# Second mixture of experts: where an expert's row transposes, its routing phase and spare matmuls stand in the queues

## Chip, core and metric

The program runs on one core of one Trainium2 chip. The metric is device time in microseconds (us) of one execution. The engines are named as in the profile: PE (TensorE, matmuls), DVE (VectorE), ACT (ScalarE), POOL (GpSimd) and SP (SyncE, which here only issues DMAs). Each engine runs its own instructions in the order in which they were queued, and waits at an instruction whose inputs are not there yet.

## What is computed

Three stages follow one another: attention, a first mixture of experts in which every token goes through all 8 experts, and a second mixture in which every token goes to one expert. Only the second mixture is touched by the change. Of the reference it is this part (N = 1152 tokens, D = 512, F = 1024, E = 8):

```python
def _moe2_ref(x, w_gate, w1, w2):
    cap = N // E                               # 144 tokens for each expert
    logits = x @ w_gate
    order = np.argsort(-logits.flatten())
    ...                                        # greedy: the best pair first; a token takes one expert,
    ...                                        # an expert takes at most cap tokens
    for e in range(E):
        mask = assigned == e
        h = np.maximum(x[mask] @ w1[e], 0.0)
        out[mask] = h @ w2[e]
```

## The kernel before

The last stage, `moe2`, works through the experts in the order in which they fill up. In this text "expert 0" is the one that fills first, and "phase p" is the routing that fills expert p. All of it is written as small operations that are handed to a planner (`Plan`); the planner keeps a model of times, always emits the operation that can start first by that model, and so fixes the order of the instructions on every engine. The operations have these names:

- `t`: the 36 last matmul groups of the first mixture (L689), whose sums DVE adds to `acc` and SP saves to the DRAM buffer `ysc`.
- Phase p, on DVE and PE in turn: `m` (each token's best open expert, L201 and L202); `bc0` to `bc2` (PE, L209: nine transposes that spread these values over the partitions); `oh` (DVE one-hots, L217 to L222); `cmp0` to `cmp8` (DVE, L229 to L232: nine compares of all tokens with all); `cnt0` to `cnt2` (PE, L241: three blocks of 27 narrow matmuls that count who stands ahead); `as`, `tot`, `close`, `left`, `sel` (who is in; which expert is full now); `pl` (PE, L302 and L304: each token's place in its expert); `spr` (DVE, L311 and L313: the one-hot matrix `hot`); `ix` (PE, L320: the token numbers in order); `ad` (DVE, L326 and L328: row addresses); `ga` (POOL, L338: two gathers of 72 rows, `xa` and `xb`, from `ysc`). `wlo` and `whi` load the expert's weights through SP (L358, L362).
- Expert p, on PE: `tin0` and `tin1` (L413, L414: transposes of the gathered rows, four each), 32 matmuls of the first layer (`h`, L422), 32 of the second (`y`, L432), `to0` and `to1` (L441: transposes back), and `sc` (POOL, L447: two scatters to `out`). ACT copies out of PSUM in between.

The main line is a list: the 36 `t`, then 64 matmuls for each expert. It is emitted in its own order. Everything else is fitted in between. `plan.mark` names a point of the main line, and an operation can be made to wait for it in the plan. Two such points matter here. Phase p may not begin (`m`) before the mark `("at", p)`, which is the main operation number HA + HB(p - 1) = 20 + 30(p - 1). And `tin0` and `tin1` of expert p wait for the gather and for `("h0", p - 1)`, which is the last matmul of the first 4 of the previous expert; from there on the planner may emit them as soon as its model says that the gather has landed. In that model a gather lands 0.9 + 1.5 us after its issue on POOL:

```python
op("m", [("close", p - 1), ("left", p - 1), ("at", p)] if p else [], ...)
op("ga", ["ad"] + ..., [("POOL", 2.1, 0.0), ("DMA", 0.9, 1.5)], gather)
op(f"tin{h}", ["ga"] + ... + ([("h0", p - 1)] if p else [("t", 35)]), ...)
plan.mark(("at", p), CFG["HA"] + CFG["HB"] * (p - 1))
```

The first gather needs all of `ysc`, so it comes after the last `t`. `ybank()` hands out four PSUM banks in turn to `t`, `tin`, `h`, `y` and `to`; `T` (three banks) serves the broadcasts and counts; `PV` is a single bank that `tot`, `pl` and `ix` share. The gathered rows have two buffers, so the gather of expert p also waits for `tin1` of expert p - 2.

Of the kernel before, what the change touches and what calls it, by code (L numbers as in the profile page):

```python
# [35 lines left out]
KT = D // 128  # L36
FB = F // 128
# [5 lines left out]
def tile_attention_moe_moe2(  # L43
# [44 lines left out]
    if dbg is not None and "acc" in dbg:  # L88
        m1.dbg = dbg["acc"]
        nc.sync.dma_start(dbg["lg"], lg)  # L90
    xst.close()
    moe2(tc, nc, ctx, ps, m1, w1b, w2b, ident, lg, ysc, out)


# [66 lines left out]
        return done  # L161


CFG = dict(CG=3, NCMP=6, HA=20, HB=30)


def moe2(tc, nc, ctx, ps, m1, w1b, w2b, ident, lg, ysc, out):
    BIG = 3.0e38
    FAR = 1.0e6
    if True:  # L170
# [3 lines left out]
        bef_b, edge, meta, ones_b = c2["bef_b"], c2["edge"], c2["meta"], c2["ones_b"]  # L174
        pen, u, rem, ac, spacer, tick = c2["pen"], c2["u"], c2["rem"], c2["ac"], c2["spacer"], c2["tick"]
        X = {}
# [3 lines left out]
        plan = Plan()  # L180
# [7 lines left out]
        S_ = {}  # L188

        def phase(p):  # L190
# [34 lines left out]
            def compare(j):  # L225
                g = two.tile([128, NT, 128], BF, name="cmp", bufs=CFG["NCMP"])
                mj = d["m"][:, j:j + 1]
                if j:
                    V.tensor_scalar(g[:, :j], d["mb"][:, :j], mj, None, op0=OP.is_lt)  # L229
                if j + 1 < NT:  # L230
                    V.tensor_scalar(g[:, j + 1:], d["mb"][:, j + 1:], mj, None, op0=OP.is_le)
                V.scalar_tensor_tensor(g[:, j], d["mb"][:, j], mj, edge, op0=OP.subtract, op1=OP.is_lt)  # L232
                d["g", j] = g
# [132 lines left out]
            def op(name, deps, segs, f, *a):  # L366
                plan.add((name, p), [x if isinstance(x, tuple) else (x, p) for x in deps], segs,
                         lambda: f(*a))

            if not last:  # L370
                op("m", [("close", p - 1), ("left", p - 1), ("at", p)] if p else [], [("DVE", 0.5, 0.15)], prefer)
                for c in range(3):
                    op(f"bc{c}", ["m"], [("PE", 0.33, 0.2)], bcast, c)
                    op(f"mb{c}", [f"bc{c}"], [("ACT", 0.37, 0.1)], bcopy, c)
                op("oh", ["m"], [("DVE", 1.35, 0.1)], onehot)
                mb = ["mb0", "mb1", "mb2"]
                for j in range(NT):
                    op(f"cmp{j}", mb, [("DVE", 1.12, 0.15)], compare, j)
                cg = CFG["CG"]
                js = [list(range(j, min(j + cg, NT))) for j in range(0, NT, cg)]  # L380
                for n, g in enumerate(js):
                    op(f"cnt{n}", ["oh"] + [f"cmp{j}" for j in g] + (["cnt0"] if n else []),
                       [("PE", 0.23 * len(g), 0.2)], count, g)
                op("as", [f"cnt{n}" for n in range(len(js))], [("DVE", 0.8, 0.1)], assign)
                op("tot", ["as"], [("PE", 0.04, 0.2)], total)
                op("left", ["as"], [("DVE", 0.4, 0.1)], left)
                op("close", ["tot"], [("DVE", 1.1, 0.1)], close)
                op("sel", ["close", "left"], [("DVE", 0.6, 0.1)], select)
            else:
                op("sel", [("sel", p - 1), ("left", p - 1)], [("DVE", 1.3, 0.1)], select)  # L390
# [4 lines left out]
            op("ix", ["spr"], [("PE", 1.0, 0.2)], index)  # L395
            op("ad", ["ix"], [("DVE", 0.5, 0.2)], address)
            op("ga", ["ad"] + ([("tin1", p - 2)] if p > 1 else []) + ([("ga", p - 1)] if p else [("save", t) for t in range(3, NT)]),
               [("POOL", 2.1, 0.0), ("DMA", 0.9, 1.5)], gather)
            op("whi", ["wlo", "ga"], [("SP", 0.3, 0), ("DMA", 7.0, 2.0)], weights, 4, 8)

        Z = {}
# [2 lines left out]
        def expert(p):  # L404
# [49 lines left out]
            def op(name, deps, segs, f, *a, main=False):  # L454
                plan.add((name, p), [x if isinstance(x, tuple) else (x, p) for x in deps], segs, lambda: f(*a), main)

            for h in range(2):
                op(f"tin{h}", ["ga"] + (["tin0"] if h else []) + ([("h0", p - 1)] if p else [("t", 35)]),
                   [("PE", 0.55, 0.2), ("ACT", 0.3, 0.15)], tin, h)
            for f in range(FB):  # L460
                for kt in range(KT):
# [11 lines left out]
        for n, (f, save) in enumerate(m1.tail()):  # L473
            plan.add(("t", n), [], [("PE", 0.645, 0.2)], f, main=True)
            if save:
                t, evac = save
                plan.add(("ev", t), [("t", n)], [("DVE", 0.67, 0.1)], evac)
                plan.add(("save", t), [("ev", t)], [("SP", 0.1, 0.0), ("DMA", 0.9, 1.6)], lambda t=t: m1.save(t))
        for p in range(E):
            phase(p)  # L480
            expert(p)
        for p in range(1, E):
            plan.mark(("at", p), CFG["HA"] + CFG["HB"] * (p - 1))
        plan.run()


# [1027 lines left out]
```

## Time and profile before

| | us |
|---|---|
| median of 3 runs | 1204.88 (1204.75 to 1207.76) |
| the profiled execution | 1208.25 |
| its span, first to last instruction | 1206.4 |
| mean granted clock of PE over the span | 0.976 of full speed |

The profile page gives for each engine its busy time, and in a view of windows the busy time of each engine in any stretch together with PEclk, the clock that was granted to TensorE as a share of full speed: 1.00 is 2.4 GHz and 0.50 is 1.2 GHz. In the timeline a bracket behind a row is the time for which the engine stood idle before it, and what it waited for. A matmul in full 32-bit precision stands in the trace as two records, so that 32 of them count as x64. The last `t` of the profiled execution ends at about 1000.6 us, the second mixture's own matmuls begin with the arrival of the first gather at 1009.24 us, and the last matmul of the last expert's second layer ends at about 1198 us.

### The profile page before, as it was taken

The numbers are of one execution on the slowest core, as the hardware profiler recorded it, in microseconds if no ns is written. First come the engines' busy times: TensorE is split into PE (matmuls) and PEld (weight loads), VectorE is DVE, ScalarE is ACT, GpSimd is POOL, SyncE is SP. The second block draws the span as 40 slices with busy tenths as digits, with TensorE's granted clock in tenths as the row PEclk, the third lists the DMA queues.
The fourth block names the chain that finished last, engine by engine and source line by source line (L and its number), as shares of the span: only waits on it lengthen the run. The fifth ranks groups of instructions, "written<-read, shape, count | busy, mean of one in ns | idle before, by whom it ended". The sixth has DMA issues, their size and how long they took to land.

```text
span 1206.4 us, 19849 instructions
## 1 busy us (share of the span) xinstructions
PE 1161.8 (96%) x7718; PEld 1048.2 (87%) x7719; DVE 788.4 (65%) x1710; ACT 415.5 (34%) x934; POOL 470.1 (39%) x428
## 2 busy tenths in 40 slices
PE   7999999999899999999999999999999997889997
PEld 4989888898889888898989898898978976889997
DVE  6999984365666666666666666658898676658300
ACT  4888885224332323233232323221211111112121
POOL 6787846215543444354345434331130001134411
PEclk8999999999899999999999999999999997879999
DMA  3232223200211121111112111241000027547930
GB/s 107 68 83 73 52 66 113 70 1 1 60 46 35 35 71 36 36 55 51 36 35 71 36 35 43 68 170 36 3 34 27 1 81 238 194 160 232 288 120 21
DMA packets 92765, 90.07 MB, mean 75 GB/s; under 512 B 26368, under 2 KB 65408, under 8 KB 92544
## 3 DMA queue, kind: packets, MB, share of 16 engines
q1 hardware_dynamic: 90336, 83.43, 22.0%
q0 software_dynamic: 2048, 4.72, 1.3%
q8 instruction: 61, 1.00, 0.4%
q10 hardware_dynamic: 288, 0.66, 0.2%
q14 instruction: 32, 0.26, 0.1%
HBM read 79.48 MB, written 4.72 MB: 70 GB/s over the span
## 4 chain that ended last, share of the span: by engine, by line
PE 81%; DVE 10%; DMA 2%; POOL 2%; issue 2%; ACT 2%; SPq 0%; POOLq 0%; DVEq 0%; ACTq 0%
PE Y L907 21%; PE T L849 18%; PE T L670 11%; PE Y L689 10%; PE T L1210 5%; PE Y L432 4%; PE Y L422 4%; PE PV L1304 3%; DVE junk L944 2%; DMA xb<-ysc,ix 2%; POOL xa L338 1%; PE S L1248 1%; PE S L1250 1%; DVE negmax L1252 1%; DVE al L1291 1%
## 5 line engine op out<-in xcount | busy, mean ns | idle before, releaser
L862 DVE TENSOR_TENSOR v<-T,v 128x256 f32<-128x256 f32 (+1 forms) x200 | 90.5, 453 | 75.8 <-PE T L849 74.5
L909 DVE SCALAR_TENSOR_TENSOR acc<-Y,pw,acc 128x512 f32<-128x512 f32 x180 | 132.3, 744 | 5.4 <-PE Y L907 2.6
L670 PE MATMUL T<-xH,wa 128*128 128x384 f32 x480 | 132.4, 337 | 0.0
L849 PE MATMUL T<-xH,wa 128*128 128x256 f32 (+1 forms) x480 | 115.4, 296 | 0.0
L849 PEld LDWEIGHTS T<-big,wb 128*128 128x128 f32 x720 | 104.3, 188 | 10.3 <-DVE v L862 3.3
L849 PE MATMUL T<-big,wb 128*128 128x256 f32 (+1 forms) x720 | 108.5, 294 | 3.1 <-DVE v L862 3.1
L689 PE MATMUL Y<-wb,hh 128*128 128x512 f32 x312 | 98.2, 396 | 1.6 <-ACT acc L696 1.6
L678 ACT ACTIVATE hh<-T 128x384 fp32r<-128x384 f32 x62 | 30.5, 492 | 185.5 <-PE T L670 185.3
L670 PEld LDWEIGHTS T<-xH,wa 128*128 128x128 f32 x480 | 87.6, 188 | 2.9
L849 PEld LDWEIGHTS T<-xH,wa 128*128 128x128 f32 x480 | 84.4, 190 | 5.1
L679 DVE SCALAR_TENSOR_TENSOR hl<-T,hh 128x384 fp32r<-128x384 f32 x62 | 34.5, 556 | 78.1 <-ACT hh L678 78.0
L670 PE MATMUL T<-xL,wa 128*128 128x384 f32 x240 | 80.6, 336 | 0.0
L849 PE MATMUL T<-xL,wa 128*128 128x256 f32 (+1 forms) x240 | 71.0, 296 | 0.0
L856 DVE SCALAR_TENSOR_TENSOR hlB<-v,hhB 128x320 fp32r<-128x320 f32 x60 | 47.5, 792 | 32.3 <-ACT hhB L855 32.3
L689 PEld LDWEIGHTS Y<-wb,hh 128*128 128x128 f32 x312 | 57.1, 188 | 11.3 <-ACT acc L696 2.1
L758 POOL TENSOR_TENSOR wa<-wraw,wa 128x512 fp32r<-128x512 f32 (+1 forms) x40 | 41.1, 1027 | 64.9 <-ACT wa L757 64.9
L777 POOL TENSOR_TENSOR wb<-wraw,wb 128x512 fp32r<-128x512 f32 x20 | 25.6, 1299 | 99.3 <-ACT wb L776 99.3
L855 ACT ACTIVATE hhB<-v 128x320 fp32r<-128x320 f32 x60 | 28.3, 472 | 104.2 <-DVE v L862 104.2
L1252 DVE TENSOR_REDUCE negmax<-S 128x1 f32<-128x576 f32 (+1 forms) x80 | 60.0, 751 | 5.4 <-PE S L1250 4.6
L777 POOL TENSOR_TENSOR wa<-wraw,wa 128x512 fp32r<-128x512 f32 x20 | 26.0, 1323 | 96.2 <-ACT wa L776 96.2
L907 PE MATMUL Y<-wa,hhB 128*128 128x512 f32 x200 | 62.9, 397 | 0.0
L907 PE MATMUL Y<-wb,hhB 128*128 128x512 f32 x200 | 62.8, 396 | 0.0
(290 smaller groups left out, 3057.5 us busy)
## 6 DMA issues: line engine op xcount, KB each, us to landing
wraw<-in_moe_w SPq DMA_DIRECT2D x56, 512.0 KB
big<-in_moe_w SPq DMA_DIRECT2D x22, 512.0 KB
wraw<-in_moe_w SPq DMA_DIRECT2D x40, 256.0 KB
wa<-in_moe_w SPq DMA_DIRECT2D x18, 512.0 KB
wb<-in_moe_w SPq DMA_DIRECT2D x12, 512.0 KB
hlk<-hlk SPq DMA_DIRECT2D x14, 320.0 KB
ysc<-acc SPq DMA_DIRECT2D x9, 256.0 KB
rawk<-in_k SPq DMA_DIRECT2D x16, 128.0 KB
```

Source lines behind the costliest of these rows:

```text
L422: nc.tensor.matmul(Z["ph"][:, f % 2], d["wa"][kt // 2][:, kt % 2, f * 128:(f + 1) * 128], Z["xg", p][:, kt], start=(kt == 0), stop=(kt == ...
L432: nc.tensor.matmul(Z["py"][:, b % 2], d["wb"][f // 4][:, f % 4, b * 128:(b + 1) * 128], Z["h", p][:, f], start=(f == 0), stop=(f == FB - 1))
L670: nc.tensor.matmul(p[:, :CH], w[:, wi, kt, (fb % 2) * 128:(fb % 2) * 128 + 128], x[:, kt, o], start=(n == 0), stop=(n == 11))
L689: nc.tensor.matmul(self.Y[c][t], a[:, o], w[:, wi, fb % 2], start=(fb == 0 and n == 0), stop=(fb == FB - 1 and n == 2))
L777: G.tensor_tensor(d["W"][:, 1, h], r[:, 2 + h], d["W"][:, 0, h].bitcast(F32), op=OP.subtract)
L849: nc.tensor.matmul(bank[:, 0:n], d[t][:, ww, b, r * 128:(r + 1) * 128], x(xw, r), start=(first and i == 0), stop=(i == 5), skip_group_chec ...
L856: V.scalar_tensor_tensor(HL[:, f, o], src, 0.0, HH[:, f, o].bitcast(F32), op0=OP.max, op1=OP.subtract)
L862: V.tensor_tensor(o, bank[:, 0:n], x, op=OP.add)
L907: nc.tensor.matmul(y, h[:, f, o], w[:, ww, f], start=(f == 0 and z == 0), stop=(f == 1 and z == 2))
L909: V.scalar_tensor_tensor(self.acc[:, t], y, self.pw[:, t, e:e + 1], self.acc[:, t], op0=OP.mult, op1=OP.add)
L1210: nc.tensor.transpose(o, i, ident[:n, :n])
L1252: nc.vector.tensor_reduce(m[0:n], p[0:n, :, :288], axis=AX.XY, op=OP.max, negate=True)
```

## The change

There are four edits, all in `moe2`:

- `("at", p)` stays for phase 1 alone. From phase 2 on a phase begins, in the plan, as soon as `close` and `left` of the phase before it are done.
- `tin0` and `tin1` of expert p > 0 wait for a new mark `("tn", p)` in place of `("h0", p - 1)`. It is the main operation 8 (LEAD) before expert p's first matmul, so the transposes stand among the last 7 matmuls of expert p - 1.
- The planner's model of a gather's flight is 5.0 us in place of 1.5 us for p > 0. This only moves operations.
- 24 matmuls `fill` (FILL) are put on the main line behind the last `t`: 128 x 512, bf16, stationary `ones_b`, moving the `hot` matrix of phase 0, all into one bank of `ybank()`. Nothing reads what they write.

```diff
--- before.py
+++ after.py
@@ -161,7 +161,7 @@
         return done
 
 
-CFG = dict(CG=3, NCMP=6, HA=20, HB=30)
+CFG = dict(CG=3, NCMP=6, HA=20, LEAD=8, FILL=24)
 
 
 def moe2(tc, nc, ctx, ps, m1, w1b, w2b, ident, lg, ysc, out):
@@ -368,7 +368,7 @@
                          lambda: f(*a))
 
             if not last:
-                op("m", [("close", p - 1), ("left", p - 1), ("at", p)] if p else [], [("DVE", 0.5, 0.15)], prefer)
+                op("m", [("close", p - 1), ("left", p - 1)] + ([("at", p)] if p == 1 else []) if p else [], [("DVE", 0.5, 0.15)], prefer)
                 for c in range(3):
                     op(f"bc{c}", ["m"], [("PE", 0.33, 0.2)], bcast, c)
                     op(f"mb{c}", [f"bc{c}"], [("ACT", 0.37, 0.1)], bcopy, c)
@@ -395,7 +395,7 @@
             op("ix", ["spr"], [("PE", 1.0, 0.2)], index)
             op("ad", ["ix"], [("DVE", 0.5, 0.2)], address)
             op("ga", ["ad"] + ([("tin1", p - 2)] if p > 1 else []) + ([("ga", p - 1)] if p else [("save", t) for t in range(3, NT)]),
-               [("POOL", 2.1, 0.0), ("DMA", 0.9, 1.5)], gather)
+               [("POOL", 2.1, 0.0), ("DMA", 0.9, 1.5 if p == 0 else 5.0)], gather)
             op("whi", ["wlo", "ga"], [("SP", 0.3, 0), ("DMA", 7.0, 2.0)], weights, 4, 8)
 
         Z = {}
@@ -455,7 +455,7 @@
                 plan.add((name, p), [x if isinstance(x, tuple) else (x, p) for x in deps], segs, lambda: f(*a), main)
 
             for h in range(2):
-                op(f"tin{h}", ["ga"] + (["tin0"] if h else []) + ([("h0", p - 1)] if p else [("t", 35)]),
+                op(f"tin{h}", ["ga"] + (["tin0"] if h else []) + ([("tn", p)] if p else [("t", 35)]),
                    [("PE", 0.55, 0.2), ("ACT", 0.3, 0.15)], tin, h)
             for f in range(FB):
                 for kt in range(KT):
@@ -476,11 +476,23 @@
                 t, evac = save
                 plan.add(("ev", t), [("t", n)], [("DVE", 0.67, 0.1)], evac)
                 plan.add(("save", t), [("ev", t)], [("SP", 0.1, 0.0), ("DMA", 0.9, 1.6)], lambda t=t: m1.save(t))
+        X["f"] = None
+
+        def fill():
+            if X["f"] is None:
+                X["f"] = m1.ybank()
+            nc.tensor.matmul(X["f"], ones_b, S_[0]["hot"].rearrange("p t c -> p (t c)")[:, 0:512],
+                             start=True, stop=True)
+
+        for i in range(CFG["FILL"]):
+            plan.add(("fill", i), [("spr", 0)], [("PE", 0.23, 0.0)], fill, main=True)
+        nf = len(plan.line)
         for p in range(E):
             phase(p)
             expert(p)
+        plan.mark(("at", 1), CFG["HA"])
         for p in range(1, E):
-            plan.mark(("at", p), CFG["HA"] + CFG["HB"] * (p - 1))
+            plan.mark(("tn", p), nf + 2 * FB * KT * p - CFG["LEAD"])
         plan.run()
```

All engines but PE keep their number of instructions; PE gets the 24 matmuls with their weight loads. The order moves from phase 1 on. Three places follow.

On PE, behind the last `t`, where the first gather is awaited. Before, the last count of phase 1 (L241) and its total (L256) are followed by the transposes of expert 0 (L413, L414):

```order
L241 LDWEIGHTS cmp_10184
L241 MATMUL T_10105<-oh_10020,cmp_10184 128x8
L256 LDWEIGHTS ones_b_2927
L256 MATMUL PV_10229<-a_10225,ones_b_2927 128x72
L413 MATMUL Y_10266<-ident_66,xa_10191 128x72
L414 MATMUL Y_10266<-ident_66,xb_10192 128x72
```

With the change the spare matmuls (L484) stand around the counts and the total: 3 ahead of the second count block, 14 ahead of the third, 5 behind it, and these last two behind the total:

```order
L256 LDWEIGHTS ones_b_2927
L256 MATMUL PV_10256<-a_10244,ones_b_2927 128x72
L484 LDWEIGHTS ones_b_2927
L484 MATMUL Y_10147<-hot_10032,ones_b_2927 128x512
L484 LDWEIGHTS ones_b_2927
L484 MATMUL Y_10147<-hot_10032,ones_b_2927 128x512
L413 MATMUL Y_10285<-ident_66,xa_10205 128x72
L414 MATMUL Y_10285<-ident_66,xb_10206 128x72
```

What moved: PE has 24 matmuls to run between the last `t` and the first transposes, of which 17 stand ahead of the third count block.

On PE, expert 1's transposes. Before, they stand in the first layer of expert 0 (L422), after 22 of its 32 matmuls, and the broadcast of phase 2 (L209) stands just ahead of them:

```order
L209 MATMUL T_10356<-ident_66,m_10339 128x128 x3
L209 MATMUL T_10360<-ident_66,m_10339 128x128 x3
L209 MATMUL T_10365<-ident_66,m_10339 128x128 x3
L422 MATMUL Y_10345<-xg_10265,wa_9986 128x144 x2
L422 MATMUL Y_10345<-xg_10265,big1_9985 128x144 x2
L413 MATMUL Y_10396<-ident_66,xa_10326 128x72
L414 MATMUL Y_10396<-ident_66,xb_10327 128x72
L413 MATMUL Y_10396<-ident_66,xa_10326 128x72
L414 MATMUL Y_10396<-ident_66,xb_10327 128x72
L422 MATMUL Y_10345<-xg_10265,wa_9986 128x144 x2
L422 MATMUL Y_10409<-xg_10265,big1_9985 128x144
```

With the change they stand in the second layer of expert 0 (L432), 7 matmuls before its end; ahead of them is the broadcast of phase 3, and between the two halves comes the index of expert 2 (L320):

```order
L209 MATMUL T_10635<-ident_66,m_10611 128x128 x3
L209 MATMUL T_10639<-ident_66,m_10611 128x128 x3
L209 MATMUL T_10644<-ident_66,m_10611 128x128 x3
L432 MATMUL Y_10607<-h_10344,wa_9988 128x144 x4
L432 MATMUL Y_10607<-h_10344,wa_9987 128x144
L413 MATMUL Y_10660<-ident_66,xa_10386 128x72
L414 MATMUL Y_10660<-ident_66,xb_10387 128x72
L413 MATMUL Y_10660<-ident_66,xa_10386 128x72
L414 MATMUL Y_10660<-ident_66,xb_10387 128x72
L320 LDWEIGHTS hot_10651
L320 MATMUL PV_10669<-meta_2925,hot_10651 72x4
```

What moved: 57 matmuls of expert 0 now stand ahead of expert 1's transposes, where 22 did, and the routing is a phase further on at that point. The same holds for the experts after it. Before, 30, 10, 4, 4, 4 and 4 of the 64 matmuls of the expert before stood ahead of the transposes of experts 2 to 7; with the change it is 57 for each.

On DVE, the address of expert 1 (L326, L328). Before, it comes right behind the one-hot matrix of expert 1 (L311, L313) and ahead of phase 2 (L201, L202):

```order
L311 SCALAR_TENSOR_TENSOR pos_10282<-sel_10246,PV_10272 128x9
L313 TENSOR_TENSOR hot_10284<-rc_2919,pos_10282 128x1296
L326 COPY idf_10318<-PV_10298 72x8
L328 SCALAR_TENSOR_TENSOR ix_10320<-idf_10318 72x4
L201 TENSOR_TENSOR lm_10338<-lg_73,pen_2929 128x72
L202 TENSOR_REDUCE m_10339<-lm_10338 128x9
```

With the change phase 2 has begun, and the address stands behind the first compare of phase 2 (L231, L232) with eight compares behind it:

```order
L220 TENSOR_TENSOR key_10336<-key_10336,km_10337 128x72
L222 TENSOR_TENSOR oh_10342<-key_10336,u_2931 128x72
L231 TENSOR_SCALAR cmp_10367<-mb_10301,m_10298 128x1024
L232 SCALAR_TENSOR_TENSOR cmp_10367<-mb_10301,m_10298,edge_2923 128x128
L326 COPY idf_10374<-PV_10348 72x8
L328 SCALAR_TENSOR_TENSOR ix_10376<-idf_10374 72x4
L229 TENSOR_SCALAR cmp_10380<-mb_10301,m_10298 128x128
```

What moved: the address of expert 1 now stands inside a run of compares, as the addresses of experts 2 to 5 do in both kernels. On POOL the gather of expert 2 now stands ahead of the scatter of expert 0, and the gather of expert 6 ahead of the scatter of expert 3; the rest of its sequence is the same.

## Rows read from the trace of the kernel before

**Rows 1.** Windows: stretch, us, busy of PE, PEld, DVE, ACT, POOL, PEclk, DMA share, GB/s
```profile
1009.24:1198.15 188.91, 176.56 (x1787) 173.73 (x1788) 81.92 (x277) 39.84 (x92) 49.69 (x48) 0.90 0.57 190
1198.15:1206.40 8.25, 1.23 (x10) 0.70 (x7) 0.00 (x0) 1.49 (x3) 1.96 (x3) 0.78 0.12 36
```

**Rows 2.** PE groups by line, 1009.24 to 1198.2: busy us, mean ns, idle before, releasers
```profile
L413 PE MATMUL Y<-ident,xa 72*128 72x72 f32 x31 | 7.2, 265 | 6.1 <-DMA xa<-ysc,ix 6.1
L414 PE MATMUL Y<-ident,xb 72*128 72x72 f32 x32 | 7.2, 272 | 6.0 <-DMA xb<-ysc,ix 6.0
L320 PE MATMUL PV<-meta,hot 128*72 128x4 bf16 x126 | 5.8, 178 | 1.1 <-DVE hot L313 1.1
```

**Rows 3.** PE timeline: start, us, what, [idle before, releaser]
```profile
1009.24 0.38 PE L414 MATMUL Y<-ident,xb 72*128 72x72 f32 x1 [0.92 <-DMA xb<-ysc,ix]
1023.54 0.28 PE L414 MATMUL Y<-ident,xb 72*128 72x72 f32 x1 [1.72 <-DMA xb<-ysc,ix]
1053.90 0.38 PE L414 MATMUL Y<-ident,xb 72*128 72x72 f32 x1 [2.67 <-DMA xb<-ysc,ix]
1078.94 0.35 PE L413 MATMUL Y<-ident,xa 72*128 72x72 f32 x1 [4.32 <-DMA xa<-ysc,ix]
```

**Rows 4.** Windows, columns as in rows 1: the five stretches at half clock
```profile
1009.24:1018.40 9.16, 9.16 (x62) 9.06 (x63) 3.53 (x11) 1.23 (x3) 1.97 (x2) 0.50 1.02 362
1025.20:1028.61 3.41, 3.41 (x40) 3.32 (x39) 3.41 (x11) 0.23 (x1) 0.00 (x0) 0.50 0.88 321
1053.90:1062.78 8.88, 8.88 (x64) 8.78 (x65) 3.58 (x21) 1.23 (x3) 0.32 (x1) 0.50 0.03 11
1079.72:1086.67 6.95, 6.95 (x56) 6.85 (x57) 1.90 (x11) 1.23 (x3) 0.73 (x2) 0.50 0.10 34
1131.04:1134.45 3.41, 3.41 (x16) 3.41 (x16) 0.34 (x2) 0.60 (x2) 2.58 (x3) 0.50 1.02 348
```

**Rows 5.** Windows, columns as in rows 1: the wait for the first gather
```profile
1000.60:1004.75 4.15, 2.19 (x55) 1.66 (x51) 3.83 (x10) 0.00 (x0) 0.06 (x1) 1.00 0.18 67
1004.75:1009.24 4.49, 0.63 (x3) 0.29 (x3) 2.85 (x16) 0.00 (x0) 2.44 (x4) 0.50 0.26 72
```

**Rows 6.** PE timeline: the last count ahead of the first gather's arrival
```profile
1004.22 0.44 PE L241 MATMUL T<-oh,cmp 128*128 128x8 bf16 x9 [0.46 <-DVE cmp L229]
```

**Rows 7.** PE timeline: the spare matmuls at the program's start
```profile
11.12 2.76 PE L1150 MATMUL PV<-wb 128*128 128x512 bf16 x6
18.07 1.04 PE L1150 MATMUL PV<-wb 128*128 128x512 bf16 x4
```

**Rows 8.** PE timeline: one sample of each block of the stage, at full clock
```profile
1173.75 8.00 PE L432 MATMUL Y<-h,wa 128*128 128x144 f32 x64
1064.05 1.15 PE L209 MATMUL T<-ident,m 128*128 128x128 f32 x9
1066.75 0.76 PE L320 MATMUL PV<-meta,hot 128*72 128x4 bf16 x18
1095.03 0.82 PE L241 MATMUL T<-oh,cmp 128*128 128x8 bf16 x27
```

**Rows 9.** DVE timeline: one routing phase, from its start to the next one's
```profile
1107.32 0.23 DVE L201 TENSOR_TENSOR lm<-lg,pen 128x72 f32<-128x72 f32 x1
1110.68 0.75 DVE L231 TENSOR_SCALAR cmp<-mb,m 128x1024 bf16<-128x1024 f32 x1
1121.98 0.23 DVE L249 TENSOR_TENSOR ok<-T,rem 128x72 f32<-128x72 f32 x1 [1.72 <-PE T L241]
1124.84 0.16 DVE L289 TENSOR_SCALAR new<-pen 128x8 f32<-128x8 f32 x1
```

**Rows 10.** POOL timeline: issues of gathers, columns as in rows 3
```profile
1044.18 1.13 POOL L338 DMA_INDIRECT xa<-ysc,ix  x1 [0.55 <-issue]
1069.06 7.28 POOL L338 DMA_INDIRECT xa<-ysc,ix  x1 [10.61 <-PE Y L432]
1113.85 7.28 POOL L338 DMA_INDIRECT xa<-ysc,ix  x1 [6.41 <-PE Y L422]
```

## The prediction

> **What bounds the kernel now.** I first read the windows view for the only part that the change touches. From the arrival of the first gather (1009.24 us) to the end of the last expert's second layer (1198.15) pass 188.91 us; PE is busy for 176.56 of them at a mean clock of 0.90, while DVE is busy for 81.92 and ACT for 39.84 [rows 1]. So this stage is a queue of PE work, and there are only two places where time can be found in it: PE standing still, and PE running at half clock. Behind it lie 8.25 us of tail (last transposes and scatters), which the change leaves alone.
>
> *PE standing still.* The groups of PE by line show who is waited for: the transposes of gathered rows stand idle for 6.1 us on `xa` and 6.0 on `xb`, the index matmuls 1.1 us on `hot` [rows 2]. Of the 12.1 us the first expert's second half has 0.92 [rows 3], which lies ahead of 1009.24. So **11.2 us** belong to the gathers of later experts; the timeline shows 1.72 at expert 1, 2.67 at expert 2's second half and 4.32 at expert 3's first [rows 3].
>
> *PE at half clock.* Five stretches of the stage ran at a granted clock of 0.50, 1.2 of 2.4 GHz: 9.16, 3.41, 8.88, 6.95 and 3.41 us, with PE busy throughout [rows 4]. Each follows a wait: the first the one for the first gather, the next three the waits of experts 1, 2 and 3, the last the 1.1 us on `hot`. Work at half clock takes twice as long, so half of each stretch is lost: 4.58, 1.71, 4.44, 3.48 and 1.71 us.
>
> The sum is made against the profiled execution, 1208.25 us, which is 3.37 above the median of 1204.88; I take the difference over to the median.
>
> **Transposes next to the last matmuls.** PE's queue is in order, so every microsecond by which the transposes stood too early was lost to all matmuls behind them. Now 57 matmuls of the expert before stand ahead, and they are the cover. How long must it be? At expert 3, POOL began the gather's issue at 1069.06 [rows 10] and PE went on at 1078.94 [rows 3]: 9.9 us, of which 7.28 are the issue of the first half [rows 10]. How long is it? The 32 matmuls of a layer take 8.00 us [rows 8], so 0.25 each. By the order, 64 matmuls and a phase stand between the index of expert 2 and its transposes: 16.0 us, plus three counts of 0.82 and a broadcast of 1.15 [rows 8], 19.6 in all, and for the later experts no less. Against 9.9 us and about 1 us for the address, 8 us are to spare. So I let the waits of experts 2 to 4 go whole, and the half-clock stretches behind them too.
>
> Expert 1 is tight. Its address now stands behind the first compare of phase 2, in a run of compares; those run from 1110.68 to 1120.26 in the phase shown (the next row's 1121.98 less its wait of 1.72) [rows 9], 9.6 us, and an issue caught in such a run ended only with it. From 1009.24: 0.6 for transposes and places (an estimate by the counts' 0.82), 3.4 for what DVE does ahead of the compares (1107.32 to 1110.68 [rows 9]), 9.6 of compares, 0.9 to come free, 1.3 for the second half's issue and 2.6 of flight (the 9.9 less 7.28): 1027.6. PE is there after 0.6, a broadcast of 1.15, an index of 0.76, 56 matmuls (14.0), three counts (2.5) and another broadcast (1.15): 1029.4. Two microseconds are little, with weights on the same DMA engines (their share was 1.02 in the first row of [rows 4]). If it lands late, the old price comes back: 1.72 and 1.71. I keep **1.5** of these 3.4; ends 0 and 3.4.
>
> Gains here: 11.2 + 1.71 + 4.44 + 3.48 = 20.8, less 1.5: **-19.3**.
>
> **Spare matmuls.** At full clock four of this shape at the program's start took 1.04 us, at half clock six took 2.76 [rows 7]; by the spacing, 0.22 and 0.43 each. 24 take 5.3 us, and from 1000.6, with two counts of 0.82, they last to about 1007.5, with some 1.8 us to go until the gather. The clock is still 1.00 up to 1004.75 and 0.50 after it [rows 5], behind a stretch in which PE was busy for 2.19 of 4.15 us. The nearest row for what is left of the wait is expert 1's 1.72 us [rows 3], which one stretch of 3.41 followed. So I expect one such stretch instead of 9.16: a gain of 4.58 - 1.71 = **-2.9**. Ends: -4.6, if the clock holds; +0.6, if it falls at 1004.75 anyway: then some 8 of them and a count take double, which ends about 0.6 behind the gather.
>
> They also hold back phase 1's last count: it ended at 1004.66 [rows 6]; now 17 spares (3.7) and two counts end at 1005.9. Its followers are hidden: the place of expert 1 stands on PE behind expert 0's transposes, which wait for 1009.24 anyway, and a total, close and select of 2.9 us (1121.98 to 1124.84 [rows 9]) with another 0.9 us for the total's wait still fit. The gather itself waits for saves on SP, which no edit touches.
>
> **Routing not held back.** This adds no work; it brings each phase's blocks up to where DVE can serve them. Does PE then wait for DVE? A phase lasts 17.5 us on DVE (1107.32 to 1124.84), of which 1.72 were a wait for PE [rows 9]. Between two broadcasts the new order has 52, 44 and 45 matmuls (13.0, 11.0, 11.3), counts 2.5, broadcast 1.15, index 0.76, place about 0.4 (half as many matmuls as the index), and in the latter two an expert's transposes, about 1.6 by their columns against the broadcast's: 17.8, 17.4 and 17.7 us. That is a near tie. Bounds: nothing, or the difference of about 1 us in each of five phases, 5 us; I take **+1.5**, as PE's own blocks are the longer ones.
>
> In the first phase the index of expert 1 now has one matmul between it and the broadcast; `hot` is ready some 2 us after the places, PE earlier: **+0.6**, and no more than the 1.1 us that the same wait had at the end [rows 2]. That last wait of 1.1 us, with its stretch of 1.71, stays: the last two places and indices still follow each other through the one bank. Ends: -2.8 to 0.
>
> **Gather's model and tail.** A number in the planner costs nothing; the two gathers that moved ahead of a scatter on POOL put the scatters back by an issue, at places where the next user of their rows is an expert away.
>
> Sum: -19.3 - 2.9 + 1.5 + 0.6 = **-20.1**. Of the profiled 1208.25 that makes 1188.2, of the median **1184.8**.
>
> **Rivals.**
> 1. *Routing becomes the pace.* For it: the tie above, and PE now arrives early at 15 count blocks. Against it: DVE is busy 81.92 of 188.91 us [rows 1]. If PE is 2 us late in each of five phases and expert 1's wait stays: +8.5 and +1.9, **1195**.
> 2. *The transposes still wait.* Routing now runs on, so each gather's issue falls into compares; experts 2 to 4 would have to land 8 us later than before. Issues of 7.28 us at experts 3 to 5 speak for it (two of the three are shown), the 1.13 us at expert 2, also among compares, against it [rows 10]. Then only the spares' -2.9 and the +0.6 are left: **1202.6**. The Trainium skill (SBUF — State Buffer, section "SBUF: two separate sides") says that GpSimd cannot write the descriptors of its DMAs while VectorE runs an instruction that takes the port pair both share. By that rule this edit works against itself; three of four issues agree, one does not. Held for a whole run of compares, 9.6 us, a gather would still come before PE at experts 2 to 7; by the rule it is expert 1 that pays its 3.4 us in full, 1186.7, which lies inside the forecast's range (0.1 of its 0.76).
> 3. *Slower: the clock stays down.* Half-clock stretches went on although PE was busy for 8.88 of 8.88 us [rows 4], so work alone does not end them at once. If the clock falls at the first gather and stays down for two phases' work (35 us), the waits' 11.2 less 3.6 are still won and the old 15.9 of clock, but 35 are lost: 1204.9 - 7.6 - 15.9 + 35 = **1216**. It decides once half clock lasts over about 47 us in sum, where it was 31.8. Against it: from 1028.61 until expert 2's wait the old order was at full clock, routing blocks and all, as the gap in [rows 4] shows.
>
> **How the numbers follow.** Chances: the forecast 0.76, with its own range of 1177 to 1190; routing as the pace 0.13; transposes still waiting 0.07; the clock 0.04. The range from the lowest end (all waits and clock gone, with -2.8 and -4.6: 1176.7, put at 1176) to rival 1 is 1176 to 1196. A measurement of this kernel can tell about 0.3% from no change, 3.6 us; 1202.6 lies within it. Faster: 0.76 + 0.13 + half of rival 2, 0.92; same 0.04; slower 0.04.
>
> **What would show it.** Right: idle of PE before L413 and L414 behind expert 0 near zero, but for expert 1; half-clock stretches at one or two places, not five; the time from the first gather's arrival to the last layer near 169 us. Wrong: idle on `hot` or compares (L241) of over 3 us, idle at expert 2 or later on a gather, or a half-clock stretch inside the routing without a wait ahead of it.

## The result: the changed kernel's time and its profile

| | before | after |
|---|---|---|
| median, us | 1206.32 (1204.75 to 1210.87, 4 runs) | 1188.01 (1186.08 to 1190.19, 4 runs) |
| profiled execution, us | 1208.25 | 1186.11 |
| its span, us | 1206.4 | 1184.3 |

The ratio of the times is 0.984, with a 95% interval of 0.981 to 0.988. Executions of one kernel lie 1.6 to 7.2 us apart. One thing that differs between them stands ahead of anything changed: a stretch of 3.41 us at half clock near 970 us, in the first mixture, stands in 9 of the 14 profiles of this document and not in the others. So beside the medians I compare one length in the profiles, **the stage**: from PE's first transpose of `xb` of expert 0 to the first transpose back (L441) behind the last expert's matmuls. Before, it is the 188.91 us of [rows 1].

Windows of after (columns as in rows 1): the stage, the tail, the half-clock stretch in the stage, and the wait for the first gather.
```profile
1011.55:1176.01 164.46, 162.35 (x1788) 160.69 (x1789) 81.35 (x275) 40.22 (x92) 55.97 (x48) 0.99 0.66 218
1176.01:1184.30 8.29, 1.23 (x10) 0.70 (x7) 0.00 (x0) 1.49 (x3) 1.96 (x3) 0.71 0.12 36
...
1007.42:1011.55 4.13, 0.28 (x1) 0.14 (x1) 1.77 (x12) 0.00 (x0) 2.07 (x4) 1.00 0.27 76
1012.24:1015.65 3.41, 3.41 (x30) 3.35 (x29) 3.24 (x8) 2.18 (x5) 0.00 (x0) 0.50 1.02 390
```
The stage is 24.45 us shorter. PE stands idle for 2.11 of it (164.46 less 162.35) instead of 12.35, and one stretch ran at half clock where [rows 4] show five. But it begins 2.31 us later: 1011.55 against 1009.24.

PE's waits of after from 1003 to 1180 us: line, what it waited for, us in sum, times, longest.
```profile
PE Y L413 <- DMA xa<-ysc,ix: 2.8, 1, 2.8
PE PV L302 <- DVE selb L297: 1.8, 2, 1.5
PE Y L414 <- DMA xb<-ysc,ix: 1.1, 1, 1.1
...
PE PV L320 <- DVE idf L326: 0.3, 1, 0.3
```
The timeline of PE places them.
```profile
1010.18 0.28 PE L413 MATMUL Y<-ident,xa 72*128 72x72 f32 x1 [2.76 <-DMA xa<-ysc,ix]
1011.55 0.28 PE L414 MATMUL Y<-ident,xb 72*128 72x72 f32 x1 [1.09 <-DMA xb<-ysc,ix]
1033.27 0.23 PE L413 MATMUL Y<-ident,xa 72*128 72x72 f32 x1
1048.84 0.18 PE L302 MATMUL PV<-selb,bef_b 128*128 128x9 bf16 x1 [1.54 <-DVE selb L297]
1104.97 0.76 PE L320 MATMUL PV<-meta,hot 128*72 128x4 bf16 x18 [0.26 <-DVE idf L326]
```
Both waits on a gather are the first gather's; those of later experts ([rows 2, 3]) are all gone; the row at 1033.27, expert 1's transposes, has no bracket. The place (L302) now waits, in two phases, for DVE's `selb`. The timelines of POOL and DVE tell why.
```profile
1006.99 1.15 POOL L338 DMA_INDIRECT xa<-ysc,ix  x1 [19.73 <-DVE asum L281]
1018.61 6.87 POOL L338 DMA_INDIRECT xb<-ysc,ix  x1 [0.30 <-issue]
1036.64 7.28 POOL L338 DMA_INDIRECT xa<-ysc,ix  x1 [8.35 <-PE Y L432]
...
1047.71 0.33 POOL L280 TENSOR_TENSOR ac<-ac,a 128x72 f32<-128x72 f32 x1
```
```profile
1042.74 0.34 DVE L232 SCALAR_TENSOR_TENSOR cmp<-mb,m,edge 128x128 bf16<-128x128 f32 x1
...
1044.22 0.27 DVE L251 TENSOR_TENSOR a<-oh,na 128x72 bf16<-128x72 bf16 x1
...
1048.07 0.23 DVE L294 TENSOR_TENSOR seltmp<-ac,new 128x72 f32<-128x72 f32 x1 [1.83 <-POOL ac L280]
```
Expert 2's gather issue lasts from 1036.64 to 1043.92, just past the last compare (ends 1043.08). Behind it in POOL's queue stand `xb`'s issue, expert 0's two scatters and then the small add `ac` (L280, in `left`), whose input `a` was ready at 1044.49. It starts at 1047.71; DVE's selection waits 1.83 us for it, and PE 1.54.

### The profile page after: what moved, and what is told of

Its sections match the earlier page's. It is cut to its first block, busy times and chain, and to the rows that moved or that the text cites. A ratio compares the mean times of both kernels' runs of the same rounds, so it can differ in the third digit from the quotient of the medians.

```text
span 1184.3 us, 19903 instructions
## 1 busy us (share of the span) xinstructions
PE 1151.8 (97%) x7743; PEld 1036.9 (88%) x7743; DVE 788.0 (67%) x1710; ACT 415.8 (35%) x934; POOL 475.8 (40%) x428
```

## The experiments

The table has every kernel that was run; "idle" is the stage less PE's busy time in it, "half" the stretches at a granted clock of 0.50 within the stage, waits in them included. The ratio is to executions of the kernel before that were measured together with the kernel of the row.

| kernel | median, us | ratio to before [95%] | stage | idle | half |
|---|---|---|---|---|---|
| before | 1206.3 to 1209.1 | 1 | 188.91 | 12.35 | 36.5 |
| after | 1188.01 | 0.984 [0.981, 0.988] | 164.46 | 2.11 | 3.41 |
| no spares | 1186.49 | 0.982 [0.980, 0.985] | 167.70 | 1.98 | 9.22 |
| transposes only | 1189.65 | 0.985 [0.983, 0.988] | 169.20 | 2.62 | 10.2 |
| routing only | 1208.27 | 0.999 [0.998, 1.001] | 188.63 | 17.63 | 30.9 |
| spares only | 1212.91 | 1.005 [1.003, 1.007] | 188.67 | 14.76 | 30.7 |
| add on VectorE | 1186.76 | 0.984 [0.982, 0.986] | 163.49 | 0.87 | 3.41 |
| no spares, add on VectorE | 1186.96 | 0.983 [0.981, 0.985] | 167.53 | 1.44 | 9.93 |
| one compare | 1196.74 | 0.991 [0.988, 0.994] | 173.75 | 6.56 | 10.2 |
| lead 32 | 1198.52 | 0.992 [0.990, 0.995] | 175.36 | 6.96 | 15.0 |
| 12 spares | 1189.62 | 0.986 [0.984, 0.988] | 166.96 | 2.21 | 8.02 |
| 40 spares | 1191.66 | 0.989 [0.986, 0.993] | 170.19 | 4.71 | 3.41 |
| 13 spares behind counts, add on VectorE | 1185.64 | 0.981 [0.979, 0.984] | 164.44 | 1.07 | 3.41 |
| 11 spares behind counts, add on VectorE | 1182.42 | 0.979 [0.978, 0.980] | 162.32 | 0.91 | 0 |

**Which edit carries the gain?** Four kernels undo or do parts alone.

```diff
-CFG = dict(CG=3, NCMP=6, HA=20, LEAD=8, FILL=24)      # after
+CFG = dict(CG=3, NCMP=6, HA=20, LEAD=8, FILL=0)       # no spares
```


> The changed kernel without its 24 spare matmuls. Theory A (the spares save clock at the first gather but cost as much elsewhere): the first gather's issue comes back to about 1004.7 us (1007.0 with the spares) because the last packets of the save of the last rows are not delayed, and the half-clock stretch behind the gather is 9 us or more again, so 2.1 us are won and about 2.9 lost: 1187 to 1190 in time, within 1.5 us of the changed kernel. Rival B (the spares bring their whole 2.9 us and the late issue has another cause): issue still near 1007, time 1191 or more.

```diff
-op("m", [...] + ([("at", p)] if p == 1 else []), ...)  # no spares
+op("m", [...] + [("at", p)], ...)                      # transposes only: all marks ("at", p) as before
```


> Only the transposes' new place (and the planner's 5.0 us of flight); routing held as before, no spare matmuls. Theory A (the place of the transposes carries the gain): PE's idle time at the transposes of experts 1 to 4 goes to under 1 us, half-clock stretches behind them are gone, only the one behind the first gather stays: about 20 us faster than before, 1185 to 1188. Rival B (held routing makes the gathers late, so the transposes still wait without the other edit): 6 us or more of idle time remain, 1194 or more.

```diff
-op("m", [("close", p - 1), ("left", p - 1), ("at", p)], ...)   # before
+op("m", [("close", p - 1), ("left", p - 1)] + ([("at", p)] if p == 1 else []), ...)   # routing only
```


> Only the routing that is not held back; the transposes stand early as before, no spare matmuls. Theory A: the transposes still stand ahead of their gathers' arrival, 8 us or more of idle time before them and three or more half-clock stretches: 1198 to 1208. Rival B (earlier routing brings the gathers early enough by itself): under 3 us of idle time, 1190 or less.

```diff
+        for i in range(24):                            # before, and spares only; marks moved by 24 for p > 1
+            plan.add(("fill", i), [("spr", 0)], [("PE", 0.23, 0.0)], fill, main=True)
```


> Only the 24 spare matmuls. Theory A: one half-clock stretch of 3.4 us behind the first gather in place of 9.2 us (2.9 us won), the first gather about 2 us later as in the changed kernel; the waits of experts 1 to 4 stay: 1203 to 1207, no difference that can be measured. Rival B (the spares bring 2.9 us or more): 1203 or less.

The transposes' place alone (with the planner's 5.0 us) gives 1189.65, nearly the whole gain, though just above the 1185 to 1188 expected. Without the spares the changed kernel is as fast as with them. In its windows the first stretch at half clock is back as in [rows 4], on all of PE's first 9.22 us:
```profile
1009.21:1018.43 9.22, 9.22 (x64) 9.16 (x65) 8.03 (x23) 2.49 (x6) 3.38 (x2) 0.50 0.96 349
```
That costs 4.61 us against the 1.71 of after, but the first gather is there 2.34 us earlier (1009.21 against 1011.55). The spares bring the clock and lose the gather.

Routing unheld, alone, gives nothing: it makes the gathers that PE waits for later (expert 1's second issue ends at 1023.92 us, where before's ends at 1016.76, and expert 2's at 1054.95, where before's ends at 1046.62). PE's waits of that kernel from 1010 us on:
```profile
PE Y L413 <- DMA xa<-ysc,ix: 10.1, 3, 6.0
PE Y L414 <- DMA xb<-ysc,ix: 7.0, 2, 6.2
```
Spares alone came out 0.5% slower, which I had not expected. Its profiled execution (1208.47) has the stage of before: 1.2 us less lost to the half clock behind the first gather (a stretch of 6.83 against 9.16), but expert 2's gather issue, begun 1.41 us earlier than in [rows 10], is held for 8.33 us where it took 1.13, and PE waits 4.67 us for `xa` there. Its other four runs, 1212.7 to 1214.8, have no profile, so what made them slower still is open.
```profile
1042.77 8.33 POOL L338 DMA_INDIRECT xa<-ysc,ix  x1 [1.15 <-PE Y L422]
```

**The select wait.** The add moves from POOL to DVE, with and without spares.
```diff
-                G.tensor_tensor(ac, ac, d["a"], op=OP.add)
+                V.tensor_tensor(ac, ac, d["a"], op=OP.add)
```


> The changed kernel with one edit: the add of a phase's assigned tokens to ac (L280) runs on VectorE instead of GpSimd. Theory A (the add stands in GpSimd's queue behind a gather issue that is blocked for 7.28 us, so that the selection on VectorE and then the product on TensorE wait for it): the idle time before L302, 1.8 us in the changed kernel, falls under 0.4 us, the 1.83 us before seltmp goes, and the time falls by about 1.5 us, to a median near 1186.5 and a span near 1182.7. Theory B (the selection is late because VectorE itself is late): the wait stays, with another releaser, and the time stays at 1188. The gather issues stay blocked by either.

> The changed kernel without the spare matmuls and with the add of L280 on VectorE. If both effects stand by themselves: the 1186.49 of the kernel without spares, less 1.5 for the wait before L302: 1185.0, span about 1183.7; half clock 13.65 us from the first gather's wait on, none later. If the wait before L302 is only handed on to another wait: 1186.5.

PE's waits from 1011 us on, with spares:
```profile
PE PV L302 <- DVE selb L297: 0.3, 1, 0.3
...
PE PV L302 <- issue: 0.2, 1, 0.2
```
From 1.8 to 0.5 us at L302, and the stage 0.97 shorter: the add behind the held issue was the cause, although the wait stays a little above the 0.4 expected. The medians (1186.76 against 1188.01) are too close to show it. Without spares the wait only fell from 1.5 to 0.9 and the stage by 0.17; nearer to the second guess, that most of it is handed on.

**What holds the issues.** Each of a phase's nine compares becomes one instruction with two tensor inputs; `edge` is now a bf16 row of zeros, the old edge and TINY, of which each compare takes a window.
```diff
-if j:          V.tensor_scalar(g[:, :j], d["mb"][:, :j], mj, None, op0=OP.is_lt)
-if j + 1 < NT: V.tensor_scalar(g[:, j + 1:], d["mb"][:, j + 1:], mj, None, op0=OP.is_le)
-V.scalar_tensor_tensor(g[:, j], d["mb"][:, j], mj, edge, op0=OP.subtract, op1=OP.is_lt)
+V.scalar_tensor_tensor(g, d["mb"], mj, edge[:, NT - 1 - j:2 * NT - 1 - j],
+                       op0=OP.subtract, op1=OP.is_lt)
```


> The changed kernel with another form of the compares: each of a phase's nine is one instruction with two tensor inputs (128 x 1152) instead of a scalar compare on each side (L229, L231) and a short one with two tensors (L232). Theory A (GpSimd's gather issue is held while VectorE runs the scalar compares, whose form takes a port that both share; the instruction with two tensors does not): the issues behind expert 0, 7.28 us each at experts 2 to 4, take 1 to 1.7 us each; the wait before L302 falls from 1.8 to under 0.4, and the time by 1 to 2 us, 1186 to 1187, if nine such instructions take VectorE about as long as before (near 1.3 us each, some 12 us a phase). Theory B (any unbroken run of VectorE instructions holds the issue): the issues still last as long as the run, 7 us or more, and the time is 1188 or above.

Expert 2's issues in POOL's timeline (lines are one lower here); then the groups of DVE and of PE in the stage.
```profile
1039.48 1.36 POOL L337 DMA_INDIRECT xa<-ysc,ix  x1 [9.03 <-PE T L240]
1041.14 1.01 POOL L337 DMA_INDIRECT xb<-ysc,ix  x1 [0.30 <-PE Y L440]
```
```profile
L230 DVE SCALAR_TENSOR_TENSOR cmp<-mb,m,edge 128x1152 bf16<-128x1152 f32 x45 | 60.6, 1408 | 0.0
```
```profile
L240 PE MATMUL T<-oh,cmp 128*128 128x8 bf16 x405 | 14.3, 167 | 6.0 <-DVE cmp L230 5.5 <-issue 0.4
```
DVE compares without a gap from 1038.59 to 1047.97 and yet the issues go through; no issue of this kernel took over 1.89 us. So the form of the compares is the cause, as theory A has it, and not the unbroken run of theory B; that a shared port is the reason, no run shows. Theory A's time was wrong: DVE is busy for 94.69 us of the stage instead of 81.35, the counts come late in an order of PE that was planned for faster compares, and PE waits 6.0 us for them, with a stretch at half clock behind (1064.52, 3.41 us). This is the first rival of the prediction, routing as the pace.

A hold is not the rule for every issue, nor does it need the end of the run to end. In the 13 kernels with scalar compares, 81 gather issues began inside a run of them: 52 were held, for 3.84 to 8.33 us, and 29 went through in 1.0 to 1.7 us. What decides is open: between the same compares of phase 3 the issue of before took 1.13 us ([rows 10]) and that of spares only 8.33. But each of the 52 ended 0.83 to 1.03 us behind the first pause in DVE's work, which could be as short as 0.22 us; here in 12 spares, POOL and DVE:
```profile
1019.54 3.96 POOL L338 DMA_INDIRECT xb<-ysc,ix  x1 [0.31 <-issue]
```
```profile
1022.20 0.35 DVE L232 SCALAR_TENSOR_TENSOR cmp<-mb,m,edge 128x128 bf16<-128x128 f32 x1
1022.77 0.62 DVE L229 TENSOR_SCALAR cmp<-mb,m 128x768 bf16<-128x768 f32 x1 [0.22 <-PE T L241]
```
The pause begins at 1022.55, and the issue ends at 1023.50, with three more compares of the phase still to come.

**How much cover do the transposes need?**
```diff
-CFG = dict(CG=3, NCMP=6, HA=20, LEAD=8, FILL=24)
+CFG = dict(CG=3, NCMP=6, HA=20, LEAD=32, FILL=24)
```


> The changed kernel with the transposes of an expert's rows 32 matmuls ahead of its first matmul instead of 8: 24 matmuls of 0.29 us, 7.0 us earlier. Theory A (the wait is covered by the place alone, and the cover is the time between a gather's landing and its transposes): from the changed kernel's rows expert 1's second gather ends its issue at 1025.48 and lands some 3 us later, at 1028.5, while its transposes move from 1033.27 to 1026.3, so expert 1 waits about 2.3 us again and a half-clock stretch follows (3.4 us, 1.7 lost); experts 2 and 3 land 8 to 13 us ahead and still have cover. Time 3 to 5 us over the changed kernel: 1190 to 1193. Theory B (the first order of the queues or the unheld routing keeps TensorE from waiting, not the cover): no wait before L413 or L414 behind expert 0, 1188.

Timeline of PE at expert 1, and the windows of the two stretches at half clock:
```profile
1030.99 0.28 PE L414 MATMUL Y<-ident,xb 72*128 72x72 f32 x1 [2.15 <-DMA xb<-ysc,ix]
```
```profile
1012.77:1020.94 8.17, 8.17 (x59) 8.11 (x60) 6.98 (x20) 2.29 (x5) 2.33 (x2) 0.50 0.98 361
1031.18:1038.01 6.83, 6.83 (x57) 6.65 (x57) 4.23 (x23) 0.82 (x2) 0.32 (x1) 0.50 0.12 32
```
The wait of 2.15 is the 2.3 expected, at expert 1 alone; the time is not. The stage is 10.9 us longer: idle 4.85 more (waits for DVE at L256 and L302 besides), and 15.0 us at half clock instead of 3.41, 5.8 lost. A short wait came here with more loss than itself and the stretch I had counted. The clock behind the first gather stayed down for 8.17 us here, although that wait (2.93 and 0.90) is about that of after: it fell at 1010.70, ahead of the arrival, where after's fell at 1012.24, behind it. Why, no run shows.

**The spares and the first gather.** Four kernels move the spares.
```diff
-FILL=24
+FILL=12        # 12 spares;  FILL=40 in 40 spares
```


> The changed kernel with 12 spare matmuls instead of 24. Theory A (the spares make TensorE's instruction stream longer, so that the 16 KB instruction fetch, at 1004.12 without spares and at 1002.68 with 24, falls on the packets of the last save, which the first gather waits for): the fetch comes near 1003.4, behind most of the save's packets, the save lands by 1003.8 instead of 1005.29, and the first gather is issued by 1005.5 instead of 1006.99; the clock then falls in the gather's wait, as without spares or a few us later, and the time is 1186 to 1188. Theory B (the first gather is later in proportion to the spares' number): it is issued at 1005.8.

> The changed kernel with 40 spare matmuls instead of 24. Theory A (the fetch falling on the save): the fetch moves to about 1001.7, ahead of most of the save's packets, the save lands by 1003.9, the gather is issued by 1005.6 instead of 1006.99; the 16 further spares (0.215 us each, 3.4 us) end near 1010.9, about 1 us behind the gather's arrival, and no half clock is left in the stage (1.7 us saved): span 1182 to 1184.5, median 1184 to 1187.5. Theory B (lateness in proportion to the spares): the gather is issued near 1008.5 and the time is 1189 to 1190.

```diff
-            plan.add(("fill", i), [("spr", 0)], ...)                 # add on VectorE
+            plan.add(("fill", i), [("spr", 0), ("cnt2", 1)], ...)    # FILL=13, then FILL=11
```


> The changed kernel with the add of L280 on VectorE, and 13 spare matmuls that stand behind the last count of phase 1 (L241) in TensorE's queue instead of 24 that begin at the hot rows of phase 0 and stand ahead of the last counts. Theory A (standing ahead of the counts, the spares bring TensorE's instruction fetch forward onto the packets of the last save): the fetch comes where it comes without spares, 1.2 us or more behind the save's first packet, the save takes under 1.2 us from first to last packet instead of 2.8, and the first gather is issued 1.5 to 2 us earlier; the clock falls once at the end of the counts and is back between 1008 and 1012, 1 to 2 us at half clock behind the gather's arrival. Span 1181 to 1183, median 1184 to 1186. Theory B (the fetch's moment is not set by the spares): collision or none, as it falls; with a collision the gather is 2 us late again and the span is near 1184.

> The kernel with the add of L280 on VectorE and the spares behind the last count of phase 1, with 11 spares instead of 13: the two that stood behind the first transposes and held up TensorE's own work go (0.22 us each). The time from the arrival of the first gather's second half to the end of the last y, 165.06 us with 13, is 164.3 to 164.8; the save takes under 1.2 us from first to last packet again, with the instruction fetch behind it; the median is 1184.5 to 1186, about 0.98 of the kernel before. If the fetch's moment is not set by where the spares stand, it may fall on the save again: first gather 2 us later, median near 1187.

Here the DMA view has slices of 0.1 us: in tenths the busy share of the 16 engines, then GB/s, then the instruction fetch. After from 1002 to 1006 us, then 11 spares behind the counts from 1002.5 to 1006.5:
```profile
DMA  0000099899970000000000101001000000000000
GB/s 0 0 0 0 20 348 532 307 389 348 389 267 21 0 0 0 0 0 0 0 0 0 20 0 20 0 0 20 20 20 20 20 21 0 0 0 0 0 0 0
...
q8 instruction: 1, 0.02, 2.5%
```
```profile
DMA  1000099999962000000060000000000000000000
GB/s 41 20 20 0 20 348 389 348 389 369 451 246 62 0 0 0 0 0 0 0 164 0 0 0 0 0 0 0 0 0 0 0 0 0 0 0 0 0 0 0
...
q8 instruction: 1, 0.02, 1.7%
```
The block is the last save, 128 packets of 2 KB. In the second kernel the 16 KB fetch comes 0.75 us behind it (the single 164). In after it lies inside the block (the 532 is a slice with it), takes 1.6 us (2.5% of 16 engines in 4 us), and the save's last eight packets straggle in up to 1005.3, one at a time. From the records of single packets, counted from the save's first packet:

| kernel | fetch starts | save lasts | gather issued |
|---|---|---|---|
| before; no spares; transposes only; routing only | 1.34; 1.93; 1.41; 1.43 | 0.82 to 0.83 | 2.43 |
| no spares, add on VectorE | 1.21 | 0.82 | 2.51 |
| 13 and 11 spares behind counts | 1.42; 1.57 | 0.83 | 2.43 |
| spares only; 40 spares | 1.12; 1.12 | 1.11 | 2.83; 2.70 |
| after; add on VectorE; lead 32; 12 spares | 0.19; 0.21; 0.28; 0.40 | 2.80; 2.64; 2.83; 3.09 | 4.50; 4.36; 4.53; 4.80 |
| one compare | -0.29, ends at 0.83 | 1.75 | 3.46 |

Wherever the fetch overlaps the save, the save takes 1.75 to 3.09 us and the gather is late; elsewhere it takes 0.82 to 1.11. The gather's issue follows the save's last packet by 1.59 to 1.73 us in all 14. That the fetch is what stretches the save rests on these 14 profiles; no run moved the fetch and nothing else. That the number of spares sets the fetch's moment is refuted: 12 did not move it out of the save, and 40, from which I expected it ahead of the save, had it behind. Theory B, lateness in proportion, fell too (12 spares: issued at 1007.47, not 1005.8). The times expected of both kernels were missed as well (1189.62 and 1191.66). With spares ahead of the last counts it fell into the save in five of seven profiles, without spares or with them behind the counts in none of seven. By the traces the fetch follows PE's place in its queue and not the time: counted in the trace's records of PE's matmuls and weight loads, it starts behind 11822 to 11826 of them in these seven, behind 11813 in spares only and 40 spares, and behind 11803 to 11807 in the five. What decides between the last two is open.

40 spares cost in another way: 12 of them ran behind the gather's arrival (2.6 us at 0.22), and idle grew by 2.6.

13 spares behind the counts freed the first gather, as expected, but the span of 1185.2 lies above the 1181 to 1183 expected: the last save began at 1005.52, where that of before began at 1002.26, and why the program was later up to there is open. The kernel with 11 spares is the fastest: 1182.42, below the 1184.5 to 1186 expected, and its ratio's interval [0.978, 0.980] lies below those of after and of no spares with the same add on VectorE [0.981, 0.985]; that of 13 spares overlaps it. Its windows, from the total of phase 1 to the gather and then the stage:
```profile
1006.29:1009.89 3.60, 3.12 (x9) 1.07 (x9) 3.19 (x20) 0.00 (x0) 1.33 (x3) 0.53 0.29 83
1009.98:1172.30 162.32, 161.41 (x1787) 159.33 (x1788) 81.17 (x277) 39.74 (x92) 48.42 (x43) 1.00 0.66 221
```
The clock falls while the spares run, in time that is waited away, and is back at 1009.89, before the stage's own matmuls. With 13 spares it did not fall in the wait but at 1012.68, behind the arrival, for 3.41 us. Its stage is 2.12 us longer, where 0.3 to 0.8 was expected for the two spares: the half-clock stretch, at 1.71 us lost, is most of it. The two kernels differ in two spares, and their medians by 3.2 us; how much of that is the spares and how much the clock's luck, one profile each does not tell.

## Why the prediction was right, step by step

The prediction, 1184.8 in 1176 to 1196, held: 1188.01. Its sum of -20.1 met -18.3 in medians (-16.9 from the 1204.88 that it started from) and -22.1 in profiled executions. Against the profiles, term by term:

| term | predicted | measured | |
|---|---|---|---|
| waits and half clock of experts 1 to 4 | -20.8 | -20.8 | all gone |
| kept for expert 1 | +1.5 | 0 | no wait |
| spares: the clock | -2.9 | -2.9 | one stretch of 3.41 instead of 9.16 |
| spares: the first gather | 0 | +2.1 | issued 4.50 instead of 2.43 behind the save's first packet |
| PE waits for routing | +1.5 | +1.8 | another mechanism |
| first index on `hot` | +0.6 | 0 | no wait |
| last wait on `hot` with its stretch | 0 | -2.55 | 0.26 instead of 1.10, no stretch |
| program up to the save | | +0.2 | not of the change's making as far as shown |

The measured terms add up to -22.1. That the sum came this near is partly luck: the late first gather (+2.1) and the last wait on `hot` (-2.55), both put at 0, nearly cancel.

- *Transposes.* Right in cause and size; the kernel with this edit alone has nearly the whole gain. The reserve at expert 1 was not needed: `xb`'s issue ended at 1025.48, PE came at 1033.27, 7.8 us later; the prediction had reckoned with 1.8 us between landing and PE, or 4.4 between issue and PE. That this is the expert with least cover was right: moved 24 matmuls ahead, its transposes alone waited, 2.15 us.
- *Spares.* The clock term came out exact, by luck in part: of the five profiles with 24 spares ahead of the counts two have a stretch of 3.41 us behind the first gather (after, add on VectorE), two one of 6.83 (spares only, one compare) and one 8.17 (lead 32). The step that failed is "The gather itself waits for saves on SP, which no edit touches": no edit touches the saves' order, but an instruction fetch came to lie on the save's packets. Net, the spares bring nothing here (1186.49 without them); 11 placed behind the counts do (a ratio of 0.979 against 0.983 without spares, both with the add on VectorE).
- *Routing unheld.* The size was near, the reason wrong. PE does not wait for a routing phase that is too long; two places wait for an add that stands behind a held gather issue on POOL. The prediction had the held issue among its rows but asked only when the gather lands, not what else is queued on POOL.
- *The ends on `hot`.* "That last wait of 1.1 us, with its stretch of 1.71, stays" failed: 0.26 us. It is gone with either of the other two edits alone (0.26 with routing only, 0.28 with transposes only) and stays at 1.1 with the spares only. Its lower end, -2.8, was in the range.
- *Rivals.* Routing as the pace needs a longer phase: 13 us more of DVE work made 6.0 us of waits. Transposes did not wait, although four of the sixteen issues were held for about 7 us. The Trainium skill (SBUF — State Buffer, section "SBUF: two separate sides"), named there, has GpSimd blocked from writing descriptors while VectorE runs an instruction that takes both ports; the kernel with one two-tensor compare agrees, 1.36 us against 7.28. But the same section of the Trainium skill gives the pair away for one instruction, and here an issue was held over many instructions of at most 0.75 us, or, in 29 of 81 cases, not at all. The clock did not stay down.
- *Signs.* One stretch at half clock, and no gather waits behind expert 0, as written. The stage was to be near 169 us and is 164.46: the surplus is what was kept at expert 1, on `hot` and in the last wait.

## What to carry to other kernels

Place an in-order engine's dependent work as late as its consumer allows, and take the cover from the worst issue that the trace shows, not from the usual one; that one move was the gain here. When a queue is found to be held, list everything behind the held instruction, small adds too. Work that fills a wait is better queued behind the work that the wait follows: ahead of it, it can move other things, here an instruction fetch.

## What the runs showed of the hardware

- A save of 256 KB lasted 0.9 to 2.3 us longer than 0.83 in all five profiles in which an instruction fetch of 16 KB (0.94 to 1.44 us apart from the save, 1.12 to 1.69 on it) lay on it, and at most 0.3 us longer in the other nine.
- Of 81 gather issues on POOL that began inside scalar compares on DVE, 52 were held, for 3.84 to 8.33 us, until 0.83 to 1.03 us behind the first pause in DVE's work; 29 went through in 1.0 to 1.7 us, and which ones, is open. Among two-tensor compares each took 1.0 to 1.9 us. A pause put into the compares, or compares that wait for the gather's issue, were not tried.
- Half clock that ended inside a wait cost nothing behind it: in the profile with 11 spares a stretch of 3.41 us ended at 1009.89, 0.09 us ahead of the arrival of the second half, and the stage ran at 1.00 throughout. In before the same fall, at 1004.75, lasted 9.16 us into the stage ([rows 4, 5]).
